# Retention and two feed-forward layers on one core: the opening's inputs in halves, its weights' lower halves on VectorE, and one weight converted later

## The chip, the cores and the metric

One core of a Trainium2 chip runs the whole program. Its engines are TensorE (PE: matmuls, and PEld for its weight loads), VectorE (DVE), ScalarE (ACT), GpSimd (POOL) and SyncE (SP), which here issues DMAs and relays some semaphores. The metric is the device time of one execution in microseconds; a lower time is better.

## The reference

Only what matters is kept: `retention` over 4 x 8 heads of 576 positions, then a feed-forward layer with ELU, then a gated one. Everything is float32.

```python
scores = scale * np.matmul(q, k.transpose(0, 1, 3, 2))          # 4 x 8 heads, 576 positions, 64 wide
rel = pos[:, None] - pos[None, :]
Dmat = np.where(rel >= 0, gamma[:, None, None] ** rel[None, :, :], 0.0)
x = np.matmul(scores * Dmat[None], v)                            # -> 2304 x 512
h = x @ w_in                                                     # 512 -> 2048
x = np.where(h > 0.0, h, np.exp(np.minimum(h, 0.0)) - 1.0) @ w_out
gate = 1.0 / (1.0 + np.exp(-(x @ w_gate)))                       # 512 -> 1536
out = (gate * (x @ w_val)) @ w_out2
```

## The kernel before, in words

**Retention** goes in 18 steps (`Step`) of 128 positions, all 8 heads of a step at once, in four pairs of heads (`p`, NP = 4). A step's inputs q, kT, k and v lie in one tile `in` of 1 MB (a few steps use spare space under the name `y`). POOL scales v by `vt` (`scale`, L191). PE forms the scores into the PSUM tile `ts` (`scores`) and k times v into `to` (`sums`), all at L194; DVE masks the scores into `a` (`causal`, L206). `states` carries the running state from one half step to the next: a sum into `st_half` (L227; at a sequence's first chunk a plain copy, L229), the sum at its end (L231), and a multiplication on POOL (L232). PE applies the state to q (`inter`) and the masked scores to v (`outs`); between these two, `inter` puts an empty instruction into SP's queue which waits for PE, and the first matmul of `outs` waits for that one. DVE scales the result out of PSUM (`x_scaled`, L266), ACT rounds it to the upper half of x (L271) and DVE takes the lower half (`x_low`, L274).

**Float32 products** are made of three products of rounded halves: upper x upper, upper x lower, lower x upper. `split` (L81, L82) makes the halves of a tile: ACT rounds the upper one, then the engine named as `lo_engine` subtracts it from the source for the lower one. Before the change that is POOL for all weights and for all activations g of the first layer.

**Weights** come as 64-bit words, 512 KB each. `Weight.chain` turns one into float32 halves in stages: two ACT operations (L120, L121), two on DVE (L123, L124), one on DVE (L127), one on DVE (L129), then `split`. The opening needs four of them: `weights[0]` and `weights[2]` (first layer's inputs for slices 0 and 1), `weights[1]` and `weights[3]` (their outputs). A "slice" is 128 of the inner width.

**The feed-forward pieces** run in passes of two slices (FP = 2) over all tokens. In the first pass pieces are 256 tokens wide (`ff[s]`, s = 0, 1, 2, ...): even s for slice 0, odd s for slice 1. `ups` is the product with the first weight (L290 in the first pass), ELU on ACT (L305, L306) and DVE (L309), and `finish`, which splits the result into `g`. `downs` is the product with the second weight into `acc` (L86 to L88); it runs two pieces later (LAG = 2). At the end of a group of 256 tokens ACT copies `acc` to `y` (L356).

**What sets the order** is the program itself: it is written under a manual schedule, and every engine works its instructions off in the order of the code. The opening is written out by hand (steps 0 and 1, the chains of two weights, and matmuls on zeros, `warm_up`). From s = 0 on, `block(n)` does the PE work of step n together with the scores and sums of step n + 1. At s = 1 comes `block(2)` and then the whole chain of `weights[1]`; `block(3)` follows that chain. At s = 2 come `ups` of `ff[2]`, which needs x of steps 2 and 3, `block(4)`, and `downs` of `ff[0]`, which needs `weights[1]`; `weights[3]` is converted in stages in between.

```python
            if s == 1:
                block(2)
                for _ in weights[1].chain():
                    pass
            if 0 < s < LATE:
                block(s + AHEAD)
```

**DMAs** of inputs and weights are issued by SP, small constants (`tri`, `vt`, `cq_sb`, `cs_sb`) by ACT at the start. Eight completion counters (DMAHW0 to DMAHW7 in the listings) are handed to the transfers in turn; a transfer that gets a counter is issued only when the transfer that had it before has landed. Before the change the counters fall like this: 0 first half of tri, 1 step 0's input, 2 second half of tri, 3 vt, 4 cq_sb, 5 cs_sb, 6 second piece of vt, 7 step 1's input; then 0 third piece of vt, 1 and 2 the first two weights, 3 step 2's input, and so on.

Of the kernel before, what the change touches and what calls it, by code (L numbers as in the profile page):

```python
# [15 lines left out]
ALU = mybir.AluOpType  # L16


B, H, S, D = 4, 8, 576, 64
NP = H // 2  # L20
C = 128
NC = 5
NT = B * S
# [8 lines left out]
G0 = [sum(GS[:g]) for g in range(NG)]  # L32
# [4 lines left out]
LATE = 4  # L37
# [10 lines left out]
def retention_elu_glu(  # L48
# [30 lines left out]
    def split(hi, lo, src, lo_engine):  # L79

        act.copy(hi, src)  # L81
        lo_engine.tensor_tensor(out=lo, in0=src, in1=hi.bitcast(F32), op=ALU.subtract)  # L82
# [22 lines left out]
    class Weight:  # L105
# [4 lines left out]
            self.raw = rpool.tile([128, 2 * DM], I32, tag="raw", name="raw") if raw is None else raw  # L110
            sp.dma_start(out=self.raw, in_=self.src.bitcast(I32))

        def chain(self):


            words = self.raw.rearrange("p (n two) -> p two n", two=2)
            low, up = words[:, 0, :], words[:, 1, :]
            t = tpool.tile([128, DM], I32, tag="t", name="t")
            f, u = t.bitcast(F32), t.bitcast(U32)
            act.activation(out=f, in_=up.bitcast(F32), func=AF.Abs)  # L120
            act.activation(out=low, in_=low.bitcast(U32), func=AF.Copy, scale=2.0**-29)  # L121
            yield
            dve.tensor_scalar(out=f, in0=f, scalar1=LEAST, scalar2=MOST, op0=ALU.max, op1=ALU.min)  # L123
            dve.tensor_scalar(out=u, in0=u, scalar1=5, scalar2=2, op0=ALU.logical_shift_left,  # L124
                              op1=ALU.logical_shift_right)
            yield
            dve.tensor_tensor(out=t, in0=t, in1=low, op=ALU.add)  # L127
            yield
            dve.scalar_tensor_tensor(out=u, in0=up.bitcast(U32), scalar=0xC0000000, in1=u,  # L129
                                     op0=ALU.bitwise_and, op1=ALU.bitwise_or)  # L130
            yield
            p = wpools[0] if self.i < 8 or (self.i - 8) % 12 >= 4 else wpools[1]
            w = p.tile([128, 2, DM], F32R, tag="w", name="w")
            split(w[:, 0, :], w[:, 1, :], f, pool)
            self.w = w
            yield

# [3 lines left out]
    W, weights, of_pass = {}, [], []  # L141
# [12 lines left out]
    class Step:  # L154
# [2 lines left out]

        def __init__(self, n):
            self.n, self.swept = n, None
            two, i = divmod(n, NS)  # L160
            self.last = i == NS - 1
            self.b, self.c = (2 * two, NC - 1) if self.last else (2 * two + i // (NC - 1), i % (NC - 1))
            self.g = max(g for g in range(NG) if G0[g] <= n)
            self.at = 128 * (n - G0[self.g])
# [6 lines left out]
        def load(self):  # L171
            if self.n in SPARE:
                self.t = spare_y[SPARE[self.n]].rearrange("p (q c) -> p q c", q=NP)
            else:
                self.t = inpool.tile([128, NP, 4 * C], F32, tag="in", name="in")
            self.q, self.kT, self.k, self.v = (self.t[:, :, i * C : i * C + C] for i in range(4))
            if not self.last:
                sp.dma_start(out=self.t, in_=ain[self.b, self.c].rearrange("p r x -> r p x"))
                return
            for X in range(2):  # L180
                src = ain[self.b + X, self.c]
                for i in range(2):
                    sp.dma_start(out=self.t[:, :, i * C + HC * X : i * C + HC * X + HC],
                                 in_=src[:, :, i * C : i * C + HC].rearrange("p q x -> q p x"))
                sp.dma_start(out=self.t[64 * X : 64 * X + 64, :, 2 * C :],
                             in_=src[:, :HC, 2 * C :].rearrange("p t x -> t p x"))

        def scale(self):
            v = self.v.rearrange("t p (h d) -> t p h d", h=2)
            by = vt[:, int(self.last), :].rearrange("t (p x) -> t p x", x=4)[:, :, 2:4].unsqueeze(3)  # L190
            pool.tensor_tensor(out=v, in0=v, in1=by.to_broadcast([128, NP, 2, D]), op=ALU.mult)  # L191

        def mm(self, out_, w, x, start):
            return pe.matmul(out_, w, x, start=start, stop=True, skip_group_check=True)  # L194
# [24 lines left out]
        def states(self):  # L219

            if self.last:
                self.st = st_last
                return
            self.st = st[self.n % 2], st_half
            new = to[:, :, : NP * D].rearrange("d x (p e) -> d x p e", p=NP)
            if self.c:
                dve.tensor_tensor(out=st_half, in0=self.st[0], in1=new[:, 0], op=ALU.add)  # L227
            else:
                dve.tensor_copy(st_half, new[:, 0])  # L229
            end = st_last[self.b % 2] if self.c == NC - 2 else st[(self.n + 1) % 2]  # L230
            dve.tensor_tensor(out=end, in0=st_half, in1=new[:, 1], op=ALU.add)  # L231
            pool.tensor_tensor(out=end, in0=end, in1=cs_sb.unsqueeze(2).to_broadcast([128, NP, D]), op=ALU.mult)  # L232
# [44 lines left out]
    class FF:  # L277
# [14 lines left out]
            for k in range(KB):  # L292
                mm3(h, w[:, 0, c[k]], w[:, 1, c[k]], x[:, 0, k, t], x[:, 1, k, t], k == 0, k == KB - 1)

        def finish(self, e):
            self.gt = g_tile()
            split(self.gt[:, 0, : self.n], self.gt[:, 1, : self.n], e, pool)

        def ups(self, stage, s):
            n, e = self.n, e_tile()[:, : self.n]  # L300
            h = h_bank()[:, :n]
            if self.kind == "a":
                self.up(W["i", self.f].w, h)
                stage()
                act.activation(out=e, in_=h, func=AF.Relu, scale=-1.0)  # L305
                act.activation(out=e, in_=e, func=AF.Exp, scale=-1.0)  # L306
                stage()

                dve.scalar_tensor_tensor(out=e, in0=e, scalar=-1.0, in1=h, op0=ALU.add, op1=ALU.max)  # L309
            else:  # L310
                v = tv[:, s % 2, :n]
                self.up(W["g", self.f].w, h)
                stage()
                act.activation(out=e, in_=h, func=AF.Sigmoid)  # L314
                self.up(W["v", self.f].w, v)
                stage()
                dve.tensor_tensor(out=e, in0=e, in1=v, op=ALU.mult)  # L317
            self.finish(e)

        def sums(self):  # L320

# [27 lines left out]
        def evac_a(self, sums):  # L349
            g, t = self.g, slice(self.at, self.at + self.n)  # L350
            if g not in y_of:
                y_of[g] = y_tile(g)
            y = y_of[g].rearrange("p (e t) -> p e t", e=KB)[:, :, t]
            for e, a in enumerate(sums):
                if self.P == 0:
                    act.copy(y[:, e], a)  # L356
                else:
                    dve.tensor_tensor(out=y[:, e], in0=y[:, e], in1=a, op=ALU.add)
            if self.final:
                x = x_of["b", g] = x_tile(g)  # L360
                for e in range(KB):
                    split(x[:, 0, e, :], x[:, 1, e, :], y[:, e], dve if e % 2 else pool)
# [15 lines left out]
    with tc.manual_schedule():  # L378
# [70 lines left out]
                next(chain)  # L449


        w0, w2 = weights[0].chain(), weights[2].chain()
        warm_up(WARM[0])
        steps[0].scale()
        steps[0].scores()
# [51 lines left out]
        for s in range(len(ff) + LAG):  # L507
            chain = conv[s].chain() if s in conv else None
            stage = lambda: next(chain) if chain is not None else None
            stage()  # L510
            if halves is not None:
                next(halves)
            halves = chain
            if LATE <= s < NSTEP - AHEAD:
                block(s + AHEAD)
            if s < len(ff):
                ff[s].ups(stage, s)
            else:
                stage()
                stage()  # L520
            if s == 0:
                steps[2].scores()
                steps[2].sums(True)
                steps[2].causal()
                steps[2].states()
                steps[3].scale()
            if s == 1:
                block(2)
                for _ in weights[1].chain():
                    pass  # L530
            if 0 < s < LATE:
                block(s + AHEAD)
            for w in loads.get(s, []):
                w.load()
            if s >= LAG:
                ff[s - LAG].downs(stage)
            else:
                stage()
            if s == begins[1] + LAG - 1:
                ret.close()  # L540
                wpools.append(ctx.enter_context(tc.tile_pool(name="w2", bufs=4, side="right")))
                psum["acc"] = ctx.enter_context(tc.tile_pool(name="ps_acc", bufs=4, space=bass.MemoryType.PSUM))
                ps_t = ctx.enter_context(tc.tile_pool(name="ps_t", bufs=1, space=bass.MemoryType.PSUM))
                tv = ps_t.tile([128, 2, 512], F32, name="tv")
# [70 lines left out]
```

## Time and profile before

| | us |
|---|---|
| runs shown | 1462.06, 931.27, 929.28 |
| their median | 931.27 |
| the profiled execution, whole | 931.67 |
| its span, first to last instruction | 929.9 |
| PE busy in the span | 909.7 |
| mean granted TensorE clock | 0.991 of 2.4 GHz |

A reader starts from the span and PE's busy time: they are 20 us apart. Times in the rows below count from the span's start. A timeline row gives the start, the length, the engine, the line, the operation, what it writes and reads, and in square brackets how long the engine stood before it and what ended that. Lines of a timeline are those of the kernel before.

### The profile page before, as it was taken

Reading aid. Unit: us, or ns where it says so; the run is one execution under the profiler, and the core shown is the slowest. Engines: PE = TensorE matmul, PEld = TensorE weight load, DVE = VectorE, ACT = ScalarE, POOL = GpSimd, SP = SyncE. Lnnn points to the kernel's source line nnn. Section 1 sums busy time; section 2 is a strip of 40 time slices with the busy share of each in tenths; the row PEclk is TensorE's granted clock in tenths of the full one; section 3 lists DMA queues with packets and bytes.
Section 4 is the critical chain, followed back from the end, with each engine's and each line's share of the span. In section 5 each row is a group of like instructions: output and inputs, shape, how many; then the busy total and the mean of one; then the engine's idle time right before and its main releaser. Section 6 shows DMA issues by size and latency. Waiting matters only on the chain.

```text
span 929.9 us, 15387 instructions
## 1 busy us (share of the span) xinstructions
PE 909.7 (98%) x6418; PEld 770.0 (83%) x6418; DVE 468.5 (50%) x756; ACT 365.5 (39%) x673; POOL 304.2 (33%) x264
## 2 busy tenths in 40 slices
PE   6799999999999999999999999999999999999998
PEld 5698988888888888888888888888888888888886
DVE  3767625555464555566884334444435354343223
ACT  2345465544545445545673333223223232221111
POOL 2455423332333333334563213222222233222111
PEclk8899999999999999999999999999999999999999
DMA  9566311201111111102121101111111012000113
GB/s 342 175 204 214 86 47 47 68 29 39 46 47 46 46 46 46 46 24 67 46 69 46 46 23 52 39 46 46 46 46 46 23 45 66 25 23 1 46 45 114
DMA packets 26998, 60.55 MB, mean 65 GB/s; under 512 B 6576, under 2 KB 7600, under 8 KB 26928
## 3 DMA queue, kind: packets, MB, share of 16 engines
q1 hardware_dynamic: 24864, 56.89, 19.2%
q10 hardware_dynamic: 2064, 2.67, 0.8%
q8 instruction: 50, 0.82, 0.4%
q14 instruction: 20, 0.16, 0.1%
HBM read 54.84 MB, written 4.72 MB: 64 GB/s over the span
## 4 chain that ended last, share of the span: by engine, by line
PE 95%; DVE 3%; DMA 1%; issue 1%; ACT 0%; ACTq 0%; POOL 0%; DVEq 0%; POOLq 0%
PE acc L86 12%; PE acc L87 12%; PE acc L88 12%; PE h L86 12%; PE h L88 12%; PE h L87 12%; PE tv L87 5%; PE tv L86 5%; PE tv L88 5%; PE to L194 4%; PE h L290 3%; PE ts L194 1%; DMA vt<-in_csmall 1%; DVE e L266 0%; DVE x L274 0%
## 5 line engine op out<-in xcount | busy, mean ns | idle before, releaser
L82 POOL TENSOR_TENSOR g<-e,g 128x512 fp32r<-128x512 f32 (+1 forms) x148 | 167.5, 1131 | 562.4 <-ACT g L81 522.8
L86 PE MATMUL h<-x,w 128*128 128x512 f32 (+1 forms) x520 | 192.5, 370 | 0.0
L88 PE MATMUL h<-x,w 128*128 128x512 f32 (+1 forms) x520 | 192.3, 370 | 0.0
L87 PE MATMUL h<-x,w 128*128 128x512 f32 (+1 forms) x520 | 192.3, 370 | 0.0
L81 ACT CAST g<-e 128x512 fp32r<-128x512 f32 (+1 forms) x148 | 82.6, 558 | 230.0 <-DVE e L317 154.6
L317 DVE TENSOR_TENSOR e<-e,tv 128x512 f32<-128x512 f32 (+1 forms) x60 | 38.1, 635 | 231.4 <-PE tv L88 231.4
L86 PE MATMUL acc<-g,w 128*128 128x512 f32 (+1 forms) x352 | 124.3, 353 | 0.6 <-ACT y L356 0.6
L87 PE MATMUL acc<-g,w 128*128 128x512 f32 (+1 forms) x352 | 123.9, 352 | 0.0
L88 PE MATMUL acc<-g,w 128*128 128x512 f32 (+1 forms) x352 | 123.8, 352 | 0.0
L309 DVE SCALAR_TENSOR_TENSOR e<-e,h 128x512 f32<-128x512 f32 (+1 forms) x88 | 51.9, 590 | 137.0 <-ACT e L306 136.5
L88 PEld LDWEIGHTS h<-x,w 128*128 128x128 f32 x520 | 98.0, 188 | 17.6
L86 PEld LDWEIGHTS h<-x,w 128*128 128x128 f32 x520 | 97.9, 188 | 17.7
L87 PEld LDWEIGHTS h<-x,w 128*128 128x128 f32 x520 | 97.9, 188 | 17.6
L82 POOL TENSOR_TENSOR w<-t,w 128x512 fp32r<-128x512 f32 x68 | 90.6, 1332 | 17.7 <-ACT w L81 17.6
L314 ACT ACTIVATE e<-h 128x512 f32<-128x512 f32 (+1 forms) x60 | 33.3, 556 | 154.4 <-PE h L88 147.8
L305 ACT ACTIVATE e<-h 128x512 f32<-128x512 f32 (+1 forms) x88 | 45.8, 521 | 112.1 <-PE h L88 96.7
L87 PE MATMUL tv<-x,w 128*128 128x512 f32 (+1 forms) x240 | 88.7, 370 | 0.0
L86 PE MATMUL tv<-x,w 128*128 128x512 f32 (+1 forms) x240 | 88.6, 369 | 0.0
L88 PE MATMUL tv<-x,w 128*128 128x512 f32 (+1 forms) x240 | 88.6, 369 | 0.0
L87 PE MATMUL acc<-w,g 128*128 128x512 f32 x216 | 84.6, 392 | 0.0
L86 PE MATMUL acc<-w,g 128*128 128x512 f32 x216 | 84.6, 392 | 0.0
L88 PE MATMUL acc<-w,g 128*128 128x512 f32 x216 | 84.4, 391 | 0.0
(72 smaller groups left out, 1342.6 us busy)
## 6 DMA issues: line engine op xcount, KB each, us to landing
in<-in_ain SPq DMA_DIRECT2D x12, 1024.0 KB, 6.8
raw<-in_w_in SPq DMA_DIRECT2D x16, 512.0 KB, 3.5
raw<-in_w_out SPq DMA_DIRECT2D x14, 512.0 KB, 3.5
raw<-in_w_gate SPq DMA_DIRECT2D x12, 512.0 KB, 3.5
raw<-in_w_val SPq DMA_DIRECT2D x12, 512.0 KB, 3.5
raw<-in_w_o SPq DMA_DIRECT2D x12, 512.0 KB, 3.4
y<-in_ain SPq DMA_DIRECT2D x4, 1024.0 KB, 7.6
out<-y SPq DMA_DIRECT2D x8, 256.0 KB, 2.7
```

Source lines behind the costliest of these rows:

```text
L81: act.copy(hi, src)
L82: lo_engine.tensor_tensor(out=lo, in0=src, in1=hi.bitcast(F32), op=ALU.subtract)
L86: pe.matmul(out_, wh, xh, start=start, stop=False, skip_group_check=shared)
L87: pe.matmul(out_, wh, xl, start=False, stop=False, skip_group_check=shared)
L88: pe.matmul(out_, wl, xh, start=False, stop=stop, skip_group_check=shared)
L194: return pe.matmul(out_, w, x, start=start, stop=True, skip_group_check=True)
L290: pe.matmul(h, w[:, a, c[k]], x[:, b, k, t], start=i + k == 0, stop=i == 2 and k == KB - 1)
L305: act.activation(out=e, in_=h, func=AF.Relu, scale=-1.0)
L309: dve.scalar_tensor_tensor(out=e, in0=e, scalar=-1.0, in1=h, op0=ALU.add, op1=ALU.max)
L314: act.activation(out=e, in_=h, func=AF.Sigmoid)
L317: dve.tensor_tensor(out=e, in0=e, in1=v, op=ALU.mult)
```

## The change

It has five edits. Steps 0 and 1 load their inputs in two DMAs of two pairs of heads each, and scale them in two parts (`parts`). The lower halves of `weights[0]`, `weights[2]` and `weights[1]`, and of `g` of `ff[0]` and `ff[1]`, are made by DVE instead of POOL. `block(3)` stands ahead of the chain of `weights[1]`. The copy of the state at a sequence's first chunk is on ACT instead of DVE. For the last 256 tokens of the first pass, two of the four copies of `acc` are on DVE instead of ACT.

```diff
-        def chain(self):
+        def chain(self, lo_engine=pool):
...
-            split(w[:, 0, :], w[:, 1, :], f, pool)
+            split(w[:, 0, :], w[:, 1, :], f, lo_engine)
...
+            self.parts = [slice(0, 2), slice(2, 4)] if n < 2 else [slice(0, 4)]
...
-                sp.dma_start(out=self.t, in_=ain[self.b, self.c].rearrange("p r x -> r p x"))
+                for p in self.parts:
+                    sp.dma_start(out=self.t[:, p], in_=ain[self.b, self.c, p].rearrange("p r x -> r p x"))
...
-            pool.tensor_tensor(out=v, in0=v, in1=by.to_broadcast([128, NP, 2, D]), op=ALU.mult)
+            by = by.to_broadcast([128, NP, 2, D])
+            for p in self.parts:
+                pool.tensor_tensor(out=v[:, p], in0=v[:, p], in1=by[:, p], op=ALU.mult)
...
-                dve.tensor_copy(st_half, new[:, 0])
+                act.copy(st_half, new[:, 0])
...
-        def finish(self, e):
+        def finish(self, e, lo_engine):
...
-            split(self.gt[:, 0, : self.n], self.gt[:, 1, : self.n], e, pool)
+            split(self.gt[:, 0, : self.n], self.gt[:, 1, : self.n], e, lo_engine)
...
-            self.finish(e)
+            self.finish(e, dve if self.kind == "a" and s < 2 else pool)
...
-                    act.copy(y[:, e], a)
+                    by_dve = self.at + self.n + 128 * G0[g] == NT and e % 2
+                    (dve.tensor_copy if by_dve else act.copy)(y[:, e], a)
...
-        w0, w2 = weights[0].chain(), weights[2].chain()
+        w0, w2 = weights[0].chain(dve), weights[2].chain(dve)
...
                 block(2)
-                for _ in weights[1].chain():
+                block(3)
+                for _ in weights[1].chain(dve):
                     pass
-            if 0 < s < LATE:
+            if 1 < s < LATE:
                 block(s + AHEAD)
```

DVE's order from `ff[1]`'s ELU to `ff[2]`'s, before the change (`t` is the working tile of a weight's chain, `y_104` the raw words of `weights[1]` and `weights[3]`):

```order
L309 SCALAR_TENSOR_TENSOR e<-e,h 128x256
L206 TENSOR_TENSOR a<-ts,tri 128x512
L266 TENSOR_TENSOR e<-to,cq_sb 128x2x4x64
L227 TENSOR_TENSOR y_107<-st_103,to 128x256
L231 TENSOR_TENSOR y_107<-y_107,to 128x256
L274 TENSOR_TENSOR x_108<-e,x_108 128x4x128
L123 TENSOR_SCALAR t<-t 128x512
L124 TENSOR_SCALAR t<-t 128x512
L127 ISA t<-y_104,t 128x1024
L129 SCALAR_TENSOR_TENSOR t<-y_104,t 128x512
L206 TENSOR_TENSOR a<-ts,tri 128x512
L266 TENSOR_TENSOR e<-to,cq_sb 128x2x4x64
```

and with the change, where lines 206, 227, 231, 266, 274 and 309 are 210, 231, 235, 270, 278 and 313:

```order
L82 TENSOR_TENSOR g<-e,g 128x256
L210 TENSOR_TENSOR a<-ts,tri 128x512
L270 TENSOR_TENSOR e<-to,cq_sb 128x2x4x64
L235 TENSOR_TENSOR st_103<-y_107,to 128x256
L278 TENSOR_TENSOR x_108<-e,x_108 128x4x128
L123 TENSOR_SCALAR t<-t 128x512
L124 TENSOR_SCALAR t<-t 128x512
L127 ISA t<-y_104,t 128x1024
L129 SCALAR_TENSOR_TENSOR t<-y_104,t 128x512
L82 TENSOR_TENSOR w<-t,w 128x512
L123 TENSOR_SCALAR t<-t 128x512
L124 TENSOR_SCALAR t<-t 128x512
```

The four operations of `weights[1]` now follow the mask, the scaled result, the state and the lower half of step 3 instead of standing ahead of them, a lower half of w (L82) stands behind them, and the operations of `weights[3]` follow at once.

SP's order at the start, before the change, with the counter that each issue waits for:

```order
L178 DMA in<-in_ain 128x4x512 x2
L111 DMA raw<-in_w_in 128x1024 [waits DMAHW1_49]
L111 DMA raw<-in_w_in 128x1024 [waits DMAHW2_49]
L178 DMA in<-in_ain 128x4x512 [waits DMAHW3_49]
L178 DMA y_105<-in_ain 128x4x512 [waits DMAHW4_49]
L111 DMA y_104<-in_w_out 128x1024 [waits DMAHW5_49]
L178 DMA y_106<-in_ain 128x4x512 [waits DMAHW6_49]
L111 DMA y_104<-in_w_out 128x1024 [waits DMAHW7_49]
```

and with the change:

```order
L180 DMA in<-in_ain 128x2x512 x2
L180 DMA in<-in_ain 128x2x512 [waits DMAHW0_49]
L180 DMA in<-in_ain 128x2x512 [waits DMAHW2_49]
L111 DMA raw<-in_w_in 128x1024 [waits DMAHW3_49]
L111 DMA raw<-in_w_in 128x1024 [waits DMAHW4_49]
L180 DMA in<-in_ain 128x4x512 [waits DMAHW5_49]
L180 DMA y_105<-in_ain 128x4x512 [waits DMAHW6_49]
L111 DMA y_104<-in_w_out 128x1024 [waits DMAHW7_49]
L180 DMA y_106<-in_ain 128x4x512 [waits DMAHW0_49]
L111 DMA y_104<-in_w_out 128x1024 [waits DMAHW1_49]
```

Two issues more stand ahead of the weights, and the counters shift: step 1's halves wait for the two halves of tri, the first weight for vt, the second for cq_sb, step 2's input for step 0's second half, step 3's for cs_sb, and the last two for step 1's first half and the third piece of vt. PE's order of work is the same in both.

## Rows read from the trace of the kernel before

**Rows 1.** The page: span, and TensorE's granted clock in 40 equal slices.

```profile
span 929.9 us, 15387 instructions
...
PEclk8899999999999999999999999999999999999999
```

**Rows 2.** Stretches: us, each engine's busy time, granted clock, DMA share, GB/s.

```profile
9.40:16.20 6.80, 5.55 (x146) 5.05 (x146) 1.69 (x4) 1.23 (x2) 1.81 (x3) 0.50 1.04 393
...
40.10:43.50 3.40, 3.40 (x37) 3.18 (x41) 2.84 (x4) 1.10 (x3) 1.56 (x2) 0.50 0.26 79
...
130.00:930.00 800.00, 795.47 (x3778) 664.75 (x3776) 389.79 (x619) 308.81 (x544) 246.49 (x200) 1.00 0.14 45
```

**Rows 3.** All waits of PE after 55 us: total, times, longest.

```profile
PE to L194 <- issue: 2.2, 2, 1.3
PE acc L86 <- ACT y L356: 0.6, 1, 0.6
```

**Rows 4.** Timeline of POOL, 0 to 60 us.

```profile
8.54 1.05 POOL L191 TENSOR_TENSOR in<-in,vt 128x512 f32<-128x512 f32 x1 [8.10 <-DMA vt<-in_csmall]
11.81 0.61 POOL L232 TENSOR_TENSOR st<-st,cs_sb 128x256 f32<-128x256 f32 x1 [2.22 <-DVE st L231]
...
22.25 1.50 POOL L191 TENSOR_TENSOR in<-in,vt 128x512 f32<-128x512 f32 x1
```

**Rows 5.** Timeline of PE, 0 to 55 us.

```profile
9.64 1.14 PE L194 MATMUL to<-in 64*64 64x64 f32 x32 [1.86 <-POOL in L191]
11.78 1.28 PE L194 MATMUL to<-in,y 64*64 64x64 f32 x13 [1.00 <-DVE st L231]
...
13.66 0.32 PE L194 MATMUL to<-a,in 64*64 64x64 f32 x3
...
33.38 0.27 PE L194 MATMUL to<-y,y 64*64 64x64 f32 x1 [1.61 <-DVE y L231]
...
39.32 2.81 PE L290 MATMUL h<-x,w 128*128 128x256 f32 x12 [2.98 <-ACT x L271]
```

**Rows 6.** Timeline of SP's DMA issues, 0 to 16 us.

```profile
0.73 0.99 SPq L178 DMA_DIRECT2D in<-in_ain  x2
6.30 1.14 SPq L111 DMA_DIRECT2D raw<-in_w_in  x2
...
9.73 0.38 SPq L178 DMA_DIRECT2D y<-in_ain  x1
...
11.19 0.50 SPq L111 DMA_DIRECT2D y<-in_w_out  x1
```

**Rows 7.** Timeline of DVE, 0 to 60 us.

```profile
17.44 0.46 DVE L123 TENSOR_SCALAR t<-t 128x512 f32<-128x512 f32 x1
...
18.27 0.68 DVE L274 TENSOR_TENSOR x<-e,x 128x512 fp32r<-128x512 f32 x1
...
21.57 1.27 DVE L274 TENSOR_TENSOR x<-e,x 128x512 fp32r<-128x512 f32 x1 [0.69 <-ACT x L271]
22.76 1.27 DVE L123 TENSOR_SCALAR t<-t 128x512 f32<-128x512 f32 x1
...
27.36 0.42 DVE L309 SCALAR_TENSOR_TENSOR e<-e,h 128x256 f32<-128x256 f32 x1 [1.42 <-ACT e L306]
...
34.72 1.16 DVE L124 TENSOR_SCALAR t<-t 128x512 uint32<-128x512 uint32 x1
...
37.93 0.68 DVE L266 TENSOR_TENSOR e<-to,cq_sb 128x512 f32<-128x512 f32 x1
...
43.16 0.42 DVE L309 SCALAR_TENSOR_TENSOR e<-e,h 128x256 f32<-128x256 f32 x1 [0.40 <-ACT e L306]
...
49.59 0.42 DVE L309 SCALAR_TENSOR_TENSOR e<-e,h 128x256 f32<-128x256 f32 x1 [1.42 <-ACT e L306]
```

**Rows 8.** Timeline of ACT, 0 to 60 us.

```profile
20.32 0.62 ACT L81 CAST w<-t 128x512 fp32r<-128x512 f32 x1 [0.97 <-DVE t L129]
...
27.82 0.41 ACT L81 CAST g<-e 128x256 fp32r<-128x256 f32 x1 [0.49 <-DVE e L309]
```

## The prediction

> **What bounds the kernel now.** I read the page first: the span is 929.9 us, and the granted clock is below full only in the first slices [rows 1]. The stretches come next: from 130 us to the end PE is busy for 795.47 of 800 us [rows 2], so nothing on the other engines sets the end there. All that PE waits for after 55 us is 3.4 us, most of it put down to "issue", and 0.6 us to ACT's copies of acc [rows 3]. So the change can move time only before 55 us, and whatever it moves there arrives at the end one to one, because PE then works without a pause.
>
> Before 55 us PE is not the bound but a link. It stands 1.86 us for POOL's first scaling and 2.98 us for step 3's x [rows 5], and it works at half clock in 9.4 to 16.2 us and 40.1 to 43.5 us [rows 2]. The engine to follow is DVE: every state, mask, lower half of x and ELU of the opening passes through it in the order written, and a wait of one instruction holds all behind it.
>
> I work out where each edit puts certain points of the opening, first as if the opening's start did not move, then with that.
>
> **Low halves of the first two weights on DVE.** DVE now waits in line for ACT's upper half, 0.62 us [rows 8], and makes the lower half in about 0.68 us: that price is L274's, the same subtraction on the same shape [rows 7]. Step 1's scaled result therefore comes 0.62 + 0.68 + gaps = 1.35 us later. It gets most of it back at once: L274 at 21.57 took 1.27 us and L123 at 22.76 another 1.27 us, against 0.68 and 0.46 us at 18.27 and 17.44 [rows 7]. At both places POOL was at work, once with the lower half that now leaves it and once with the scaling of 22.25 us [rows 4]. 1.35 minus 0.6 minus 0.8 leaves about nothing, so ff[0]'s ELU stays at 27.36 [rows 7]. For the second weight POOL's 1.3 us become DVE's 0.68, and nobody waits longer.
>
> The long rows are told by the trace as follows: L123 of 22.76 ends 0.28 us after POOL's instruction of 22.25 [rows 4, 7], as if it had begun only then. The Trainium skill, page "SBUF — State Buffer", section "SBUF: two separate sides", says that GpSimd and the second pair of VectorE's ports are one exclusive lock, which the first to start holds for a whole instruction. By that rule, the trace agrees, and what leaves POOL stops blocking DVE only where no scaling on POOL takes its place.
>
> **Low halves of g on DVE.** Behind ff[0]'s ELU DVE waits for ACT's rounding, 0.41 us from 27.82 [rows 8], and then works 0.42 us (the 128x256 ELU's length [rows 7]); the nearest bound above is POOL's 0.73 us for it. Step 2's mask and state are queued behind, and PE waits for the state: +0.9 us at the state of step 3, so PE's inter of step 3 goes from 33.38 [rows 5] to 34.3. The second g falls into a stand of DVE of 0.8 us and costs nothing.
>
> **block(3) ahead of weights[1].** After 34.3 PE does inter (1.05), scores (0.45) and outs (0.5, all as in later steps at full clock) and step 3's result is scaled at 36.3 instead of 37.93 [rows 7]. ACT's 0.62 us later ff[2] can start, at about 37.7 instead of 39.32, without the 2.98 us stand [rows 5] that came before the half clock of 40.1 [rows 2]. The lower half of x waits for the state behind ACT's copy (0.4) and ends at 39.1, and ff[2] ends at 40.3 instead of 42.13 (39.32 + 2.81).
>
> **What is late next.** The four operations of weights[1] took 3.5 us on DVE (L123 to L129; L124 alone 1.16 us beside POOL [rows 7]), and POOL has the same multiplication and scaling at hand in the new place. So they run from 39.0 to 42.5, ACT takes 0.62, the lower half 0.68: 43.9. The three of weights[3] follow with 1.6 us, and only then comes ff[2]'s ELU: 45.5 instead of 43.16 [rows 7], 2.3 us late. In the old order that weight's work lay where PE stood; in the new order it lies in front of an ELU. From this ELU to the next DVE had 0.8 us of stands, which shrink to none, so ff[3]'s ELU comes at about 51.2 instead of 49.59 [rows 7]: **+1.6 us**, and behind it stand the mask and the state for which PE waits at 52. Bounds: +0.5 if the two long operations meet no POOL work (1.1 us less), +2.5 if the new lower halves meet it too.
>
> **Inputs and scaling in halves.** POOL began at 8.54, when vt had landed [rows 4]. Its first half of the work costs 0.61 us by the 128x256 row at 11.81, against 1.05 for the whole [rows 4]: 0.44 us less before PE can start. When vt lands is not to be seen before the run. It cannot help before 6.3, when step 0's whole input has landed (the first weight's issue at 6.30 waits for that counter [rows 6]); and nothing in the change makes it later than 8.5. Step 1's megabyte, which before was issued at 1.2 us, right behind step 0's [rows 6], now waits for the first tri and stands about 1 us back of vt's small packets. I take 7.3, the middle. PE's sums of step 0 then start at 7.3 + 0.61 = 7.95 instead of 9.64 [rows 5]: **1.7 us earlier** (0.4 to 2.7).
>
> Two things can hold that back or add to it. First, SP: outs of step 0 waits for the empty instruction in SP's queue, which stands behind nine issues. Before, the last of them ended at 11.69, two microseconds before outs at 13.66 [rows 5, 6]. Now the second weight waits for cq_sb, which the issue at 9.73 waited for before [rows 6]; if cq_sb lands as before, six issues of 0.45 us end at 12.4, and outs is at most 1.25 us earlier. If cq_sb comes forward with vt, they end at 11.3. Second, the clock: it fell to half at 9.4 after PE had stood 1.86 us [rows 2, 5], and 5.55 us of work ran at half [rows 2]. With sums at 7.95 that stand is about 0.2 us. If the clock holds, outs and sums of steps 0 and 1 take 1.0 us instead of the 2.3 from 13.66 on, and the end of that stretch is up to 3.6 us earlier. I take it that the clock holds and that SP lets outs go at 11.7: **3.2 us earlier**, bounds 0.4 and 3.6. DVE's chain carries this through to 52 us: no later input lands too late for it (the last of the first batch is issued at 11.19 [rows 6] and is used after 30 us).
>
> **The small edits.** The state's copy goes from DVE (0.42) to ACT (0.38): nothing, ACT is idle there. The two copies of acc on DVE can save part of the 0.6 us that PE waits [rows 3], but DVE has a weight operation in front: 0, at most -0.3.
>
> **The sum.** -3.2 + 1.6 = -1.6 us on the profiled execution's 931.67, that is 930.1. This execution lies 0.4 above the median of 931.27, so 929.7.
>
> **Rivals.**
>
> *The opening hardly moves and DVE's load decides: slower.* vt's small packets may be paced by their own ring, not by step 1's. Then POOL starts at 8.4, PE stands nearly as long as before, the clock falls again, and only the 0.44 us of the first half are won: -0.4 + 1.6 = +1.2, about 932.5. For it speaks that vt is only the third of seven transfers on ACT's ring; against it, that step 1's transfer was beside it all the time. It decides as soon as the opening's gain is under 1.6 us.
>
> *SP holds outs back.* The halves put two issues more in front and cq_sb lands as before: outs only 1.25 us earlier at half clock, +0.35 us, 931.6. The Trainium skill, "SBUF — State Buffer", section "Summary: rules for kernel authors", tells to use one DMA of 128 partitions and not several, which would speak against the halves; here the rate alone doesn't show it, as the stretch 9.4 to 16.2, with transfers of 512 KB and of 1 MB, moved 393 GB/s [rows 2].
>
> *More of both.* POOL stays out of DVE's way (+0.5) and the start gains 3.6: -3.1, about 928.2. That the change doesn't reach the end at all is not likely: no pause is left behind 55 us to swallow it.
>
> **How the numbers follow.** Forecast 0.45, slower through DVE 0.28, SP 0.15, more of both 0.12. The range goes from the best of these with the runs' own scatter (the two undisturbed runs are 2 us apart, so 1 us down), 927.2, to the worst bounds, -0.4 + 2.5 = +2.1, 933.4. A measurement of this kernel tells about 2%, 18.6 us, from no change; no case comes near it, so "within 2%" has nearly all: 0.98, and 0.01 for each side.
>
> **What would show it.** In the profile of the changed kernel: POOL's first scaling at about 7.3 (under 8.0 right, 8.4 wrong); the granted clock full in 9.4 to 16.2; ff[2]'s start without a stand near 3 us; DVE without a pause from step 3's lower half of x to ff[2]'s ELU, with L82 on DVE behind 0.6 us stands for ACT; PE waiting for weights[1]'s lower half before downs of ff[0]. Wrong is the prediction if DVE's operations of weights[1] come out at half their length, if a late step's input is waited for, or if PE finds a new pause after 55 us.

## The result, and the profile after

The changed kernel takes 936.12 us (median of four runs, 935.18 to 936.64) against 931.27 before (931.46 if the disturbed run of 1462 us is counted; the ratio leaves that run out): ratio 1.0051, 95% interval 1.0039 to 1.0063. It is about 4.7 us slower, where 1.6 us faster was forecast. The profiled execution of the changed kernel took 935.79 us.

The page first: span, and granted clock in 40 slices.

```profile
span 934.0 us, 15388 instructions
...
PEclk7899999999999999999999999999999999999999
```

The span is 4.1 us longer. As before, only the first two slices show less than nine tenths of the full clock. One stretch of [rows 2] comes next, and the two in the opening in which the clock was at half (the columns are those of [rows 2]).

```profile
9.40:16.20 6.80, 2.70 (x87) 2.37 (x89) 0.69 (x1) 1.20 (x2) 1.56 (x3) 0.58 0.96 362
```

```profile
10.50:24.20 13.70, 8.31 (x156) 6.43 (x156) 6.85 (x11) 3.59 (x6) 2.41 (x3) 0.50 1.03 389
...
41.30:48.10 6.80, 6.37 (x121) 6.03 (x122) 5.77 (x10) 2.90 (x6) 2.04 (x2) 0.50 0.38 79
```

Between 9.4 and 16.2 us PE does half of the work that it did there before (2.70 against 5.55 us). The clock is at half for 13.7 and 6.8 us. Of before's two half-clock stretches in [rows 2] the first lasted 6.8 us and the second 3.4; one more of 3.4 us, from 23.0 on, has no row there.

What PE, POOL and SP do in the opening (timelines; SP's are its issues, and an issue's length includes any time that SP stands inside it):

```profile
6.48 1.19 POOL L195 TENSOR_TENSOR in<-in,vt 128x256 f32<-128x256 f32 x2 [6.04 <-DMA vt<-in_csmall]
```

```profile
7.16 1.02 PE L198 MATMUL to<-in 64*64 64x64 f32 x32
9.13 0.79 PE L198 MATMUL to<-in,y 64*64 64x64 f32 x13 [0.95 <-DVE st L235]
...
11.27 0.71 PE L198 MATMUL ts<-in 64*64 64x64 f32 x16 [0.94 <-DMA in<-in_ain]
15.13 1.13 PE L198 MATMUL to<-a,in 64*64 64x64 f32 x32 [3.16 <-SPq L251]
...
36.16 0.27 PE L198 MATMUL to<-y,y 64*64 64x64 f32 x1 [1.61 <-DVE y L235]
...
40.40 0.74 PE L294 MATMUL h<-x,w 128*128 128x256 f32 x4 [1.46 <-ACT x L275]
41.73 2.07 PE L294 MATMUL h<-x,w 128*128 128x256 f32 x8 [0.59 <-DVE x L278]
```

```profile
7.58 0.54 SPq L180 DMA_DIRECT2D in<-in_ain  x1
8.16 0.65 SPq L180 DMA_DIRECT2D y<-in_ain  x1
8.85 0.74 SPq L111 DMA_DIRECT2D y<-in_w_out  x1
9.64 2.16 SPq L180 DMA_DIRECT2D y<-in_ain  x1
11.84 3.18 SPq L111 DMA_DIRECT2D y<-in_w_out  x1
```

The first half of the story goes even better than forecast: vt has landed by 6.48 (8.54 in [rows 4]), and PE's sums of step 0 start at 7.16 instead of 9.64 [rows 5]. Then it turns. SP's issues, 0.38 to 0.50 us where [rows 6] shows them singly, grow from 0.54 to 3.18 us. The last one ends at 15.02, and outs of step 0, which waits for the empty instruction behind it, starts at 15.13: 1.5 us later than the 13.66 of [rows 5], 3.16 us after PE was ready. Is it a counter that SP stands for? The waits of SP say no; in this stretch only the two parts of tri and PE hold it up by a semaphore:

```profile
SPq L180 <- DMA tri<-in_csmall: 4.1, 2, 3.0
SPq L180 <- PE to L198: 1.2, 1, 1.2
```

The first row belongs to step 1's two halves, the second to an issue behind outs. The last issue's 3.18 us stand in the instruction itself. Before the change the same view has waits between the issues, two of them of about 1 us:

```profile
SPq L178 <- DMA vt<-in_csmall: 1.0, 1, 1.0
SPq L178 <- DMA cq_sb<-in_cq: 0.9, 1, 0.9
```

They are gone now, since vt and cq_sb come early. cq_sb, issued at 2.8 us, took 6.9 us to land before (9.7); now it lands at 6.7:

```profile
L414 ACTq DMA_DIRECT2D cq_sb<-in_cq x1: 442/442/442, 2.6 to 2.6; - x1
...
DMA to landing us min/median/max: 4.1/4.1/4.1
```

From there the delay doesn't stay 1.5 us. PE's inter of step 3 comes at 36.16 (33.38 in [rows 5]), ff[2] starts at 40.40 (39.32). Its ELU is then late on two engines:

```profile
45.19 0.62 ACT L81 CAST w<-t 128x512 fp32r<-128x512 f32 x1 [3.45 <-DVE t L129]
45.72 0.68 ACT L120 ACTIVATE t<-y 128x512 f32<-128x512 f32 x1
46.30 0.68 ACT L121 ACTIVATE y<-y 128x512 int32<-128x512 uint32 x1
46.87 0.36 ACT L309 ACTIVATE e<-h 128x256 f32<-128x256 f32 x1
```

```profile
24.89 0.69 DVE L278 TENSOR_TENSOR x<-e,x 128x512 fp32r<-128x512 f32 x1 [0.68 <-ACT x L275]
25.49 0.42 DVE L123 TENSOR_SCALAR t<-t 128x512 f32<-128x512 f32 x1
...
48.06 0.41 DVE L313 SCALAR_TENSOR_TENSOR e<-e,h 128x256 f32<-128x256 f32 x1
...
53.50 0.42 DVE L313 SCALAR_TENSOR_TENSOR e<-e,h 128x256 f32<-128x256 f32 x1 [1.42 <-ACT e L310]
```

ff[2]'s product ended at 41.73 + 2.07 = 43.80, but ACT has weights[1]'s upper half and two operations of weights[3] queued ahead and takes the ELU up at 46.87. DVE does its part at 48.06 (43.16 in [rows 7]), 4.9 us late. ff[3]'s comes at 53.50 (49.59), 3.9 us late, and that is what arrives at the end.

After 55 us PE waits about as before [rows 3], 3.6 us in all:

```profile
PE to L198 <- issue: 2.5, 2, 1.6
PE acc L86 <- ACT y L361: 0.6, 1, 0.6
```

The other 0.5 us are one more stand of 0.3 marked "issue" and 0.2 for a state.

So there are two suspects: outs held back by SP (theory A says that this and the load that the other edits put on ACT and DVE are two causes that add up), and the load alone (rival B: a late opening is swallowed by PE's later stands).

### The profile page after: what moved, and what is told of

It is laid out like the page before. It is cut to its first block, busy times and chain, and to the rows that moved or that the text cites. A ratio compares the mean times of both kernels' runs of the same rounds, so it can differ in the third digit from the quotient of the medians.

```text
span 934.0 us, 15388 instructions
## 1 busy us (share of the span) xinstructions
PE 910.8 (98%) x6418; PEld 770.3 (82%) x6418; DVE 469.4 (50%) x759; ACT 365.7 (39%) x675; POOL 298.4 (32%) x261
## 4 chain that ended last, share of the span: by engine, by line
PE 93%; DVE 3%; SPq 1%; ACT 1%; issue 1%; DMA 1%; ACTq 0%; DVEq 0%
PE acc L86 12%; PE acc L87 12%; PE acc L88 12%; PE h L86 12%; PE h L88 12%; PE h L87 12%; PE tv L87 5%; PE tv L86 5%; PE tv L88 5%; PE to L198 3%; PE h L294 2%; PE ts L198 1%; DMA tri<-in_csmall 1%; SPq L111 1%; DVE e L270 0%
## 5 line engine op out<-in xcount | busy, mean ns | idle before, releaser
L82 POOL TENSOR_TENSOR g<-e,g 128x512 fp32r<-128x512 f32 (+1 forms) x146 | 165.8, 1135 | 565.5 <-ACT g L81 525.9
L82 POOL TENSOR_TENSOR w<-t,w 128x512 fp32r<-128x512 f32 x65 | 86.6, 1332 | 8.9 <-ACT w L81 8.7
```

## Experiments

All ratios are to the kernel before, run alongside, with 95% intervals; 0.001 is 0.93 us. A quotient of two medians can differ from the ratio given by up to 0.0008.

**The halves alone, and the change without them.** The first is the kernel before plus the inputs and scaling of steps 0 and 1 in halves, the second the changed kernel with this line:

```diff
-            self.parts = [slice(0, 2), slice(2, 4)] if n < 2 else [slice(0, 4)]
+            self.parts = [slice(0, 4)]
```

> The kernel before with nothing but the halves of the inputs and of the scaling of steps 0 and 1. Theory A: outs of step 0 start near 15.1 us as in the changed kernel (13.66 before), because SP's last issue stands in front of the empty instruction, and PE's clock falls for longer: +1.5 us at the end (ratio to before 1.0016, anything from 1.0008 to 1.003). Rival B: a late outs is swallowed by PE's later stands (2.98 us before ff[2]) and the whole loss is DVE's: 0 us (0.9995 to 1.0005).

> The changed kernel without the halves (the other four edits stay). Theory A: the loss that is left is DVE's, +1.6 to +2.5 us against before (ratio 1.0017 to 1.0027), outs of step 0 start at 13.7 as before. Rival B: +4 us (1.0043).

Measured: halves alone 1.0017 (1.0007 to 1.0028), without the halves 1.0029 (1.0018 to 1.0040). The sum, 1.0046, is the change's 1.0051 within the intervals; rival B's 1.000 and 1.0043 lie outside them, the second by little. With the halves alone outs of step 0 are even later:

```profile
16.47 1.13 PE L198 MATMUL to<-a,in 64*64 64x64 f32 x32 [3.53 <-SPq L251]
```

**The last issue behind the empty instruction, and step 1 whole.** Of the changed kernel:

```diff
-        weights[3].load(raws[:, 1, :])
...
         steps[0].inter()
+        weights[3].load(raws[:, 1, :])
```

> The changed kernel with SP's last issue of the first batch (weights[3]) moved behind the empty instruction that outs of step 0 waits for. Theory A: outs of step 0 start at 12.0, as soon as the scores of step 1 are done, instead of 15.13; the end comes 2 to 3 us earlier than the changed kernel's (ratio to before 1.001 to 1.002). Rival B: outs move, the end doesn't (1.0045).

The other leaves `n < 1` in place of `n < 2` in the line of `parts`.

> The changed kernel with step 1 whole, only step 0 in halves: one issue less in front of the empty instruction. Theory A: if the number of issues and of bytes in flight holds SP, its last issue ends earlier than 15.0 and outs start at 12 to 14; ratio to before 1.001 to 1.003. Rival B: 1.0045.

Measured: 1.0037 (1.0023 to 1.0051) and 1.0049 (1.0037 to 1.0062). Both missed theory A's numbers, and neither excludes rival B's 1.0045. The traces say why. With the last issue moved, the one before it, which still stands ahead of the empty instruction, took 3.1 us:

```profile
9.27 3.12 SPq L180 DMA_DIRECT2D y<-in_ain  x1
12.52 3.13 SPq L111 DMA_DIRECT2D y<-in_w_out  x1
```

```profile
12.51 0.69 PE L198 MATMUL to<-a,in 64*64 64x64 f32 x32 [1.51 <-SPq L251]
```

Outs moved from 15.13 to 12.51, tied to whatever issue is the last ahead of them. That the end moved with them is not clear of noise here: 1.0037 and the change's 1.0051 overlap. In this profiled execution (931.0 us span) the clock stayed full throughout; its time, 932.80, is the lowest of five, and the others lie at 934.1 to 935.2. One issue less (step 1 whole) changed nothing: outs at 15.49, behind a last issue of 4.41 us, which came after a counter wait of 0.7 us. So SP stands at the issues of step 4's input and weights[3] (here at the second alone), and both have to leave.

**Both issues late, with and without halves, and with the whole change.**

```diff
-        steps[4].load()
-        weights[3].load(raws[:, 1, :])
...
         steps[0].inter()
+        steps[4].load()
+        weights[3].load(raws[:, 1, :])
```

Before plus the halves plus this:

> The kernel before with the halves, and SP's last two issues of the first batch (step 4's input and weights[3]) behind the empty instruction. If SP's full queue is what the halves cost: outs of step 0 start at 12.0 to 12.5 us (16.47 with the halves alone, 13.66 before) and the ratio to before falls from 1.0017 to 0.997 to 0.999. If the halves cost something else (transfers about 1 us later), outs move and the ratio stays at 1.001 to 1.002.

Before plus this alone, as a control:

> The control: the kernel before, inputs whole, with the same two issues behind the empty instruction. Theory A: SP didn't hold outs before (its last issue ended at 11.69, outs started at 13.66), so nothing is won: ratio 0.9995 to 1.0005, and the 1.9 us of the run with halves and late issues are the halves'. Rival: the late issues themselves bring it, 0.997 to 0.999.

The whole change plus this:

> The whole change with SP's last two issues of the first batch behind the empty instruction. Theory A (two separate causes that add): the halves then gain 1.9 us, as they do alone, and the moved chain and lower halves cost 2.7 us: +0.8 us against before, ratio 1.000 to 1.0015. Rival B (the earlier opening is of no use once DVE is loaded, its order sets the time): 1.002 to 1.003.

Measured: 0.9980 (0.9971 to 0.9989), 0.9997 (0.9988 to 1.0006) and 1.0017 (1.0006 to 1.0028). The halves turn from +0.0017 to -0.0020 when the two issues stand behind the empty instruction, and moving these issues brings nothing without halves. The kernel with halves and late issues is the fastest of the study, 929.96 against 931.31 us (medians). Its outs start with no stand in front, and SP still spends its time in the same two issues, where now only outs of step 1 meets it, for 0.36 us:

```profile
12.18 0.65 PE L198 MATMUL to<-a,in 64*64 64x64 f32 x32
...
16.46 0.70 PE L198 MATMUL to<-a,in 64*64 64x64 f32 x32 [0.36 <-SPq L251]
```

```profile
10.30 2.60 SPq L180 DMA_DIRECT2D y<-in_ain  x1
12.94 2.74 SPq L111 DMA_DIRECT2D y<-in_w_out  x1
```

With the halves alone these two issues began at 10.18 and 13.15, nearly the same times. So the transfers hardly moved; what moved is the empty instruction in front of outs, and that decides between loss and gain. By what the halves then gain 1.9 us is less clear. In the control's profiled execution, whose clock was full from 6 to 37 us, outs start only 0.36 us later than the 12.18 above:

```profile
12.54 0.22 PE L194 MATMUL to<-a,in 64*64 64x64 f32 x1
```

An earlier start and a clock that falls less often are both open as the source of the gain.

In the whole change the same move wins 0.0034 (from 1.0051 to 1.0017, intervals apart), about as much as alone (0.0037). Outs start at 12.45, hardly earlier than with one issue moved, but without the stand of 1.51 us:

```profile
12.45 1.08 PE L198 MATMUL to<-a,in 64*64 64x64 f32 x32
```

That the two causes add in full isn't decided: 1.0017 lies between theory A's range and rival B's, its interval reaches into both, and it is above the centre that additivity gives (1.0029 - 0.0020 = 1.0009).

**The scaling alone in two parts**, the inputs whole:

> The kernel before with only the scaling of steps 0 and 1 in two parts, the inputs in whole transfers, so that SP's order and counters stay as before. By the prediction's price PE's sums of step 0 start 0.44 us earlier and vt lands at 8.1 to 8.4 as before: ratio 0.9993 to 1.0. Rival: vt comes early for this too, and 1 to 2 us are won: 0.998 to 0.999.

Measured 0.9998 (0.9987 to 1.0009). POOL's first half still had to wait for vt, and PE's sums of step 0 started at 9.45, against 9.64 in [rows 5]. So the halves' gain needs the split transfers: with them step 1's megabyte no longer stands right behind step 0's, and vt lands 2 us earlier.

**The other edits one by one**, each on the kernel before. First block(3) ahead of the chain:

```diff
                 block(2)
+                block(3)
                 for _ in weights[1].chain():
...
-            if 0 < s < LATE:
+            if 1 < s < LATE:
```

> The kernel before with block(3) ahead of the chain of weights[1] and nothing else (all lower halves on POOL, inputs whole). Theory A: ff[2] starts without most of its 2.98 us stand, but its ELU on ACT and DVE now queues behind the chain and comes 2 us late; +0.5 to +1.5 us at the end (ratio 1.0005 to 1.0016), the three DVE edits share the loss of 2.7 us. Rival B: this move alone carries it, 1.0025 to 1.003. Rival C: the earlier ff[2] wins, 0.998 to 0.9995, and the lower halves cost all.

Then the lower halves on DVE, one of these three lines in each kernel: of the first two weights, of g, and of weights[1] in its old place:

```diff
+        w0, w2 = weights[0].chain(dve), weights[2].chain(dve)
...
+            self.finish(e, dve if self.kind == "a" and s < 2 else pool)
...
+                for _ in weights[1].chain(dve):
```

> The kernel before with the lower halves of weights[0] and weights[2] on DVE and nothing else. Theory A: 0.7 us later at ff[0]'s end, since DVE stands for ACT's upper half with step 1's result behind it; ratio 1.0003 to 1.001. Rivals B: 1.0000. Rival C: 1.001 or more.

> The kernel before with the lower halves of g of ff[0] and ff[1] on DVE and nothing else. Theory A: DVE stands 0.41 us for ACT's rounding and works 0.42 us with step 2's mask and state behind it, PE's inter of step 2 or 3 is 0.9 us later, the stand of 2.98 us before ff[2] doesn't swallow it; ratio 1.0008 to 1.0012. Rival B: 1.0000. Rival C: 1.001 or more.

> The kernel before with the lower half of weights[1] on DVE and nothing else. Theory A: in the old order the chain lies where PE stands 2.98 us for step 3's x; DVE's stand for ACT and 0.68 us come in front of step 3's mask and result: +0.7 to +1.3 us (ratio 1.0007 to 1.0014). Rival: the half is ready 0.6 us earlier than on POOL and nobody waits behind it: 0.9993 to 1.0003.

Measured: block(3) ahead 1.0017 (1.0006 to 1.0027); first two weights 1.0012 (1.0003 to 1.0020); g 1.0016 (1.0007 to 1.0025); weights[1] in its old place 1.0023 (1.0013 to 1.0033). Each is slower by itself, and each centre lies above its theory A. For block(3) ahead, rival B's 1.0025 is inside the interval, but as the other three are slower too, it doesn't carry the loss alone. Their sum, 1.0068, is more than the 1.0029 that the change costs without halves, so here they don't add: the last one alone stands in front of step 3's x, and block(3) ahead takes it out of that place.

With block(3) ahead (old lower halves), PE's waits show the trade:

```profile
36.76 1.95 PE L290 MATMUL h<-x,w 128*128 128x256 f32 x12 [1.46 <-ACT x L271]
...
41.63 0.39 PE L86 MATMUL acc<-g,w 128*128 128x256 f32 x1 [0.62 <-ACT w L81]
...
42.99 0.38 PE L88 MATMUL acc<-g,w 128*128 128x256 f32 x1 [0.85 <-POOL w L82]
...
46.86 0.27 PE L194 MATMUL to<-in,y 64*64 64x64 f32 x1 [0.98 <-DVE st L231]
```

The stand of 2.98 us before ff[2] [rows 5] becomes 1.46, and three new ones of 0.62, 0.85 and 0.98 us follow: 3.91 in all. PE now waits for weights[1] and, behind the late ELU, for step 5's state.

With weights[1]'s lower half on DVE in the old order, PE's stand before ff[2] grows from 2.98 to 4.35 us, by DVE's 0.68 us for ACT and its own 0.69 (the stretch has the columns of [rows 2]):

```profile
38.35 2.93 PE L290 MATMUL h<-x,w 128*128 128x256 f32 x12 [4.35 <-ACT x L271]
```

```profile
35.76 0.69 DVE L82 TENSOR_TENSOR w<-t,w 128x512 fp32r<-128x512 f32 x1 [0.68 <-ACT w L81]
```

```profile
37.36:44.19 6.83, 5.84 (x100) 5.61 (x104) 5.15 (x9) 2.96 (x6) 2.85 (x3) 0.50 0.21 54
```

Behind this longer stand the clock was at half for 6.83 us, where before it was for 3.4 [rows 2].

Not tried alone: the state's copy on ACT and the two copies of acc on DVE. PE's wait of 0.6 us for the copies of acc is unchanged.

## Why the prediction was wrong

**The step that failed: "I take it that the clock holds and that SP lets outs go at 11.7: 3.2 us earlier, bounds 0.4 and 3.6".** Outs went at 15.13. The case that came is the one priced by "If cq_sb comes forward with vt, they end at 11.3": cq_sb landed at 6.7 us, and SP's last issue still ended at 15.02. The issues were priced at 0.45 us by rows of a queue in which counter waits kept them apart; these waits vanished, and single issues took up to 3.18 us. The runs put the halves at +0.0017 (+1.6 us) instead of -3.2 us, and at -0.0020 (-1.9 us) once SP was out of the way. The bounds excluded a loss for this term with no reason that the trace gave. A second thing was missing: PE's scores of step 1 stand in front of outs and now wait for that step's second half (0.94 us at 11.27; 1.18 us in the kernel with halves and late issues), so outs start at 12.18 even with SP out of the way.

**The rival had the place and the wait, not the cause.** "SP holds outs back" was tied to cq_sb landing as before, which it didn't. It gave outs 1.25 us earlier, had 0.15 of the chance and a total of +0.35 us. No row before the change showed a long issue.

**vt at 7.3, PE's sums at 7.95**: right in kind, and too cautious; 6.48 and 7.16. **The whole clock from 9.4 to 16.2**: wrong, 0.58. It was at half from 10.5 on, after PE's stand of 0.95 us at 8.2 and within the one of 0.94 us, so before the stand for SP began at 11.97; that stand can have kept it there, not brought it there. In the whole change with both issues late, where no such stand follows, it was at half from 11.6 to 15.0 us and then full. That the clock follows from PE's first stand alone isn't so either: in the control PE stood 1.72 us there, 1.86 before, and the clock stayed full.

**DVE's load, +1.6 (0.5 to 2.5)**: right in direction, too small by its centre. Without the halves the change costs 1.0029, 2.7 us (1.7 to 3.7). The profiled executions of this kernel and of the control can be compared, as each had 3.4 us at half clock in its opening, though not at the same place: ff[2]'s ELU on DVE comes 3.1 us later (44.22 against 41.10; 2.3 was priced) and ff[3]'s 2.3 us (49.65 against 47.35; 1.6 was priced). The prediction looked for the late ELU in DVE's queue only; ACT, in its own queue, took it up first after the rounding of weights[1] and two operations of weights[3]. "ff[2] without the 2.98 us stand" was half right: 1.46 + 0.59 us are left.

**The lower halves of the first two weights, "leaves about nothing"**: the rows came out as told. L278 at 24.89 and L123 at 25.49 now take 0.69 and 0.42 us instead of 1.27 each in [rows 7], while POOL has nothing to do from 20.02 to 32.09; L124 at 19.14, beside POOL's scaling of 18.79 to 20.02, takes 1.15 us instead of the 0.43 at 25.95 and ends 0.27 us behind it. So the exclusive lock of the Trainium skill, "SBUF — State Buffer", section "SBUF: two separate sides", agrees with the trace again. Yet alone these lower halves cost 1.0012. In that run's trace PE stands 3.42 us for step 1's x in front of ff[0]:

```profile
21.72 2.93 PE L290 MATMUL h<-x,w 128*128 128x256 f32 x12 [3.42 <-ACT x L271]
```

The same view of the kernel before has two shorter stands:

```profile
21.59 0.73 PE L290 MATMUL h<-x,w 128*128 128x256 f32 x4 [1.20 <-ACT x L271]
22.89 2.00 PE L290 MATMUL h<-x,w 128*128 128x256 f32 x8 [0.57 <-DVE x L274]
```

**The lower halves of g, +0.9**: 1.0016, in its interval (0.7 to 2.3 us).

**"One to one" to the end**: it held in the changed kernel (3.9 us at ff[3]'s ELU, 4.1 at the end), but not everywhere. In the profiled execution of the halves alone, ff[3]'s ELU came 2.5 us late and the end only 0.7:

```profile
52.10 0.42 DVE L313 SCALAR_TENSOR_TENSOR e<-e,h 128x256 f32<-128x256 f32 x1 [1.42 <-ACT e L310]
```

There the two longer stands of 2.2 us marked "issue" [rows 3] were missing:

```profile
PE h L294 <- issue: 0.9, 1, 0.9
PE acc L86 <- ACT y L360: 0.6, 1, 0.6
```

The rule that was weighed against the halves (the Trainium skill, "SBUF — State Buffer", section "Summary: rules for kernel authors", one DMA and not several) is for transfers bound by DMA. The rate hardly changed (384 GB/s from 10.0 to 24.2 us in the changed kernel, 393 before), so it doesn't decide this case: the halves are the better choice in the fastest kernel, and the worse one where SP's queue stands in front of PE.

**What stays open.** What SP's long issues wait for. In the changed kernel the second weight was issued at 7.1 and took 7.9 us to land, at 15.0, and the last issue ended at 15.02:

```profile
L111 SPq DMA_DIRECT2D raw<-in_w_in x2: 430/448/467, 6.6 to 7.1; - x2
...
DMA to landing us min/median/max: 6.3/7.1/7.9
```

The same pair of times agrees within 0.1 us in the five other kernels with halves. But before the change the last issue ended at 11.69 with that weight landing at about 12.7 by the same view, so it isn't the rule by itself. A limit on what may be outstanding is argued, not shown. Nor is it shown that the missing waits make the issues long and not the larger number of transfers: the six kernels with halves differ in both from the others, whose last issue took at most 0.51 us. Nor was it settled why the clock fell in some executions of one kernel and not in others; the scatter of about 2 us up and down within one kernel goes with it.

## What to carry to other kernels

If an engine that others wait for also issues transfers, the relay (here the empty instruction that PE waits for) goes in front of every issue that isn't needed yet: an issue can hold its queue for microseconds with no semaphore in sight (up to 4.41 us here), and a change that lets SP issue sooner can bring this about. Before moving work off an engine, look for each place where the new engine stands for a third one (0.68 us for ACT here, each time), and for the queues of that third one as well. An edit that can gain (halves, -1.9 us with the two issues late) can hide in a change that loses. Running each edit alone shows which ones lose, but the halves alone lost too: it took their trace, and a run with SP out of the way, to find the gain.

## What was not expected of the hardware

SP's issue of a 512 KB transfer took 0.50 us in one kernel and 3.18 us in another. The same bytes were queued ahead of it, steps 0 and 1 in two transfers each, and the four issues before it began 0.8 to 1.6 us earlier. And PE stood for "issue" in the middle of a group of matmuls where it ran ahead: 1.81 us in the whole change with late issues.

```profile
37.83 0.56 PE L198 MATMUL to<-y 64*64 64x64 f32 x20 [1.81 <-issue]
```

A transfer of kind "instruction" (16 KB) ran from 35.27 to 36.26 us there, 1.57 us before PE went on. In the kernel before, one ran from 93.51 to 94.44 us, and PE's stand of 1.3 us ended at 95.78. That PE's own instructions were late at these places would fit both; no run here tests it.
